# Gate weights turned by PE transposes beside the first attention units, and a drain of GpSimd in the half tile

## The chip, the cores and the metric

One core of one Trainium2 chip runs the whole kernel. A core has five engines with queues of their own: TensorE (PE, matmuls; PEld are its weight loads), VectorE (DVE), ScalarE (ACT), GpSimd (POOL) and SyncE (SP), which here only issues DMAs. POOL issues DMAs too, on a queue of its own. The metric is the device time of one execution in microseconds (us), smaller is better.

## What is computed

Three layers in a row, all in float32, for 4 x 448 = 1,792 tokens. Attention with a sigmoid in place of the softmax (12 heads of 64), then a layer with three weight matrices and an elementwise maximum, then a layer of 8 experts of which each token takes one:

```
attn = sigmoid(scale * q @ k.T - log(S));  x = attn @ v          # (1792, 768)
h = max(max(x @ w1, x @ w2), x @ w3);      x = h @ w_out         # 768 x 768 each
logits = x @ w_gate + modality_bias[modality_id]                 # w_gate: (768, 8)
e = argmax(logits);  gate = softmax(logits)[e]
out = gate * (relu(x @ ew1[e]) @ ew2[e])                         # 768 -> 1024 -> 768
```

## The kernel before

PE works through four stages in order: attention, the three projections (line 457), the output product (line 523), and the experts (lines 775 and 796, then the half tile, lines 928 and 938). Float32 products are made as three products of rounded parts: each operand is split into a rounded part and the rest, which is what the many pairs of a copy and a subtraction are for (`split_qk`, `split`, `evac_X`).

The attention has 24 units of two heads, and its loop runs over 12 pairs j of them, with units A = 2j and B = 2j + 1, and once more to finish. In an iteration PE makes the scores of A (`emit_qk`), the product with v of the unit before (`emit_av`, line 320, and `emit_av_last`, line 328, for the last 64 rows of a pair), the last scores of the pair (`emit_qk_last`, line 310), the scores of B and the product of A. In between stand, in this order, the loads of units A + 4 and B + 4 on SP's queue (`load_qk`, line 254, and `load_v`), the splits of units A + 2 and B + 2 on DVE (`split_qk`, lines 275 and 276, which write `kq`), and, from j = 2 on, 2.5 us of `background` work: the loads of the projection weights (`load_chunk`, line 216, tiles `stage`) and their conversion on DVE. PE, ACT, DVE and SP run in exactly the order written (`tc.manual_schedule`); POOL's order is the framework's, its waits too.

In iteration j = 4 SP issues four more transfers, of which the second is a transpose of the gate weights by a DMA of single elements, from `w_gate` (768 x 8) to `wgT` (8 x 768) in DRAM. `wgT` is read much later: `gate_load(e)`, in the projections, reads one row for all partitions, and DVE multiplies `w_out` with it, so that the logits can be had from `h` ahead of the output product. `mb` is the bias of the modalities, broadcast to 128 partitions, and `midi` is the modality of each token, 1,792 numbers of 8 bytes. The memory that the change uses is `K1`: before, it holds `v4`, the v of two units, and later `gk`, which is three times 768 columns.

At the end, the last tile of the experts has 128 rows (the half tile, i = NF). Its first products stand at line 928, its second products at line 938, and POOL scatters its rows to `out` (`scatter`, line 804), as it did those of the tile before. A loop over further tiles (line 949) isn't entered with these inputs. What the engines do at the program's end is shown under line 1000.

Of the kernel before, what the change touches and what calls it, by code (L numbers as in the profile page):

```python
# [28 lines left out]
def attn_moe_kernel(  # L29
# [15 lines left out]
    nc = tc.nc  # L45
    B, HP, D, _, _, S = qk.shape
    NT, DM = out.shape
    E, _, FF = ew1.shape
    KB = DM // 128
# [25 lines left out]
    def hold(tag, name, *shape):  # L75
        return pool.tile([128, *shape], F32, tag=tag, name=name)

    def r(ap):
        return ap.bitcast(F32R)

    def cut(a, off, *shape):

        n = 1
        for s in shape:
            n *= s
        a = a[:, off:off + n]
        if len(shape) == 2:
            a = a.rearrange("p (a b) -> p a b", a=shape[0])
        elif len(shape) == 3:
            a = a.rearrange("p (a b c) -> p a b c", a=shape[0], b=shape[1])  # L90
        return a
# [10 lines left out]
    NW = 2 * NJ  # L102
# [5 lines left out]
    kq = [cut(kq_, 4 * S * i, 2, 2, S) for i in range(2)]  # L108
    u1, u2, u3 = (hold(f"U{i}", f"u{i}", 2048) for i in range(3))
    qk_in = [cut(u, 2 * S * i, 2, S) for u in (u1, u2) for i in range(2)]  # L110
    v4 = hold("K1", "v4", 2, NW + 1, D)
    v_in = [cut(u3, (NW + 1) * D * i, NW + 1, D) for i in range(4)] + [v4[:, i] for i in range(2)]

    stage = [hold(f"S{i}", f"stage{i}", KB * 256).bitcast(I32) for i in range(2)]
# [7 lines left out]
    wgT = dram.tile([E, DM], F32, name="wgT")  # L122
# [3 lines left out]
    ident = cpool.tile([128, 128], F32, name="ident")  # L126
# [21 lines left out]
    def ps(tag, shape, name):  # L148
        return psum.tile(shape, F32, tag=tag, name=name)
# [3 lines left out]
    def ps_a(shape, name):  # L153
        a_n[0] ^= 1
        return psum.tile(shape, F32, tag=f"a{a_n[0]}", name=name)
# [54 lines left out]
    def load_chunk():  # L210
        i = loaded[0]
        if i < len(chunks):
            kind, a, b = chunks[i]
            loaded[0] += 1
            src, n = chunk_src(a, b) if kind == "w" else (woi[a * 128:(a + 1) * 128, :].rearrange("p (a c) -> p a c", a=1), 1)
            nc.sync.dma_start(out=stage[i % 2].rearrange("p (a c) -> p a c", a=n), in_=src)  # L216
# [34 lines left out]
    def load_qk(u):  # L251
        b, hp = divmod(u, HP)
        for h in range(2):
            nc.sync.dma_start(out=qk_in[u % 4][D * h:D * (h + 1)], in_=qk[b, hp, :, h])  # L254

    def load_v(u):
        b, hp = divmod(u, HP)
        vt = v_in[u % 6]
        if u % 2 == 0:
            nc.sync.dma_start(out=vt, in_=v[b, hp])  # L260
            return

        nc.sync.dma_start(out=vt[:, 0:NW], in_=v[b, hp, :, 0:NW])
        for h in range(2):
            nc.sync.dma_start(out=vt[SR * (1 - h):SR * (2 - h), NW], in_=v[b, hp, SR * h:SR * (h + 1), NW])

    def split_qk(u):
        src, kt = qk_in[u % 4], kq[u % 2]
        if u == 0:
            nc.vector.tensor_copy(out=r(kt[:, 0, 0]), in_=src[:, 0])  # L270
            nc.scalar.activation(out=r(kt[:, 0, 1]), in_=src[:, 1], func=ACTF.Copy)
            for i in range(2):
                nc.vector.tensor_tensor(out=r(kt[:, 1, i]), in0=src[:, i], in1=kt[:, 0, i], op=ALU.subtract)
        else:
            nc.vector.tensor_copy(out=r(kt[:, 0]), in_=src)  # L275
            nc.vector.tensor_tensor(out=r(kt[:, 1]), in0=src, in1=kt[:, 0], op=ALU.subtract)
# [3 lines left out]
    def scores():  # L280
        s_n[0] += 1
        return ps(("a0", "a1", "t")[s_n[0] % 3], [128, 2, 512], "s")

    def sigmoid(dst, s):
        nc.scalar.activation(out=dst, in_=s[:, :, 0:S], func=ACTF.Sigmoid, scale=qscale, bias=nlns)  # L285

    def emit_qk(u):

        kt = kq[u % 2]
        for g in range(NJ):  # L290
            s = scores()
            for n, (a, x) in enumerate(((0, 0), (0, 1), (1, 0))):
                for h in range(2):
                    p = slice(D * h, D * (h + 1))
                    nc.tensor.matmul(s[:, h, 0:S], r(kt[p, a, 0, 128 * g:128 * (g + 1)]), r(kt[p, x, 1]),  # L295
                                     start=(n == 0), stop=(n == 2))
            sigmoid(atb[u % 2][:, 2 * g:2 * g + 2], s)

    def quarter(i, h):

        return slice(SR * (h ^ i), SR * ((h ^ i) + 1))

    def emit_qk_last(j):

        s = scores()
        for i in range(2):
            src = qk_in[(2 * j + i) % 4]
            for h in range(2):
                p = slice(D * h, D * (h + 1))
                nc.tensor.matmul(s[quarter(i, h), i, 0:S], src[p, 0, 128 * NJ:], src[p, 1], start=True, stop=True)  # L310
        sigmoid(atl[j % 2], s)
# [3 lines left out]
    def emit_av(u):  # L315
        X_t[u] = ps(f"x{u % 2}", [128, 512], "X")
        vt, at = v_in[u % 6], atb[u % 2]
        for g in range(NJ):
            for h in range(2):
                nc.tensor.matmul(X_t[u][64 * h:64 * h + 64, 0:S], vt[:, 2 * g + h], at[:, 2 * g + h],  # L320
                                 start=(g == 0), stop=False)

    def emit_av_last(j):
        for i in range(2):
            u = 2 * j + i
            for h in range(2):
                p = quarter(i, h)
                nc.tensor.matmul(X_t[u][64 * h:64 * h + 64, 0:S], v_in[u % 6][p, NW], atl[j % 2][p, i],  # L328
                                 start=False, stop=True)

    def evac_X(u):
        b, hp = divmod(u, HP)
        src = X_t.pop(u)[:, 0:S]
        dR = xR[hp][:, b * S:(b + 1) * S]
        dL = xL[hp][:, b * S:(b + 1) * S]
        nc.vector.tensor_copy(out=r(dR), in_=src)
        nc.vector.tensor_tensor(out=r(dL), in0=src, in1=dR, op=ALU.subtract)

    with tc.manual_schedule(engines={mybir.EngineType.PE, mybir.EngineType.Activation, mybir.EngineType.DVE, SP}):
        load_qk(0)  # L340
        nc.vector.memset(gw, 0.0)
        nc.vector.memset(ones, 1.0)
        make_identity(nc, ident)
# [35 lines left out]
        for j in range(NU // 2 + 1):  # L379
            A, B, more = 2 * j, 2 * j + 1, j < NU // 2  # L380
            if more:
                emit_qk(A)
            if j:
                emit_av(B - 2)
                emit_av_last(j - 1)
                evac_X(A - 2)
                evac_X(B - 2)
            if not more:
                break
            emit_qk_last(j)  # L390
            for u in (A + 4, B + 4):
                if u < NU:
                    load_qk(u)
                    load_v(u)
            if A + 2 < NU:
                split_qk(A + 2)
            if j == 1:
                load_chunk()
            if j == 4:
                nc.sync.dma_start(out=slots.rearrange("(p c) o -> p (c o)", p=128), in_=idx)  # L400
                with nc.allow_non_contiguous_dma(reason="small"):
                    nc.sync.dma_start(out=wgT, in_=w_gate.rearrange("d e -> e d"))
                nc.sync.dma_start(out=mb, in_=m_bias.partition_broadcast(128))  # L403
                nc.sync.dma_start(out=midi, in_=mid.bitcast(I32).rearrange("(i p t) -> p i t", p=128, t=2))
            if j >= 2:
                background(2.5, stop=(1, 0))
            emit_qk(B)
            emit_av(A)
            if B + 2 < NU:
                split_qk(B + 2)  # L410
# [491 lines left out]
        for p, (i, n) in enumerate(todo[:NF * NCH]):  # L902
# [9 lines left out]
            else:  # L912
                f = n - 2 * KB
# [10 lines left out]
        for g in range(2):  # L924
            acc = ps_a([128, 4, 128], "hacc1")
            for f in range(4):
                for kk in range(KB):
                    nc.tensor.matmul(acc[:, f], raw[i % 2][0][kk // 2][:, kk % 2, 128 * (4 * g + f):128 * (4 * g + f + 1)],
                                     ht[:, kk], start=(kk == 0 and f == 0), stop=(kk == KB - 1 and f == 3))
            dR, dL = hv[0][:, 4 * g:4 * g + 4], hv[1][:, 4 * g:4 * g + 4]  # L930
            nc.scalar.activation(out=r(dR), in_=acc, func=ACTF.Relu)
            nc.vector.scalar_tensor_tensor(out=r(dL), in0=acc, scalar=0.0, in1=dR, op0=ALU.max, op1=ALU.subtract)
        o = [ps("t", [128, 512], "oh0"), ps("x0", [128, 512], "oh1")]
        for f in range(FB):
            w = bufs.pop((i, 2 * KB + f))
# [5 lines left out]
        d = xo[xo_n[0] % 3]  # L941
# [7 lines left out]
    with tc.For_i(NSTAT, nreg, 1) as iv:  # L949
        nc.sync.dma_start(out=idx2, in_=slots.rearrange("(p c) o -> p (c o)", p=128)[:, bass.ds(iv * 2, 2)])  # L950
        nc.sync.dma_start(out=e_dyn, in_=exd[0:1, bass.ds(iv, 1)])
        e = nc.values_load(e_dyn[0:1, 0:1], engines=(SP,), min_val=0, max_val=E - 1)
# [51 lines left out]
```

## Time and profile before

| | |
|---|---|
| median of 3 runs | 807.19 us (807.14 to 807.71) |
| the profiled execution | 807.75 us, its span 806.0 us |
| mean granted clock of TensorE | 0.974 |
| busy: PE, DVE, ACT, POOL | 760.3, 448.5, 258.6, 65.2 us |
| DMA | 88.04 MB, mean 109 GB/s |
| DMAs that POOL issues | 59: 14 to `slots`, 30 gathers to `xg`, 15 scatters to `out` |

The span is the time from the first to the last instruction that the profile shows. The 40 slices of the page are 20.15 us each; a digit is the busy share in tenths, and 9 is 90% or more. A matmul's end is modelled, so a busy PE is not a PE at its peak. In a timeline a row is: start us, duration us, engine, line, operation, tiles (out<-in), shapes, count, and in brackets the idle time before it and what ended it. An engine's name with a q (SPq, POOLq) is its sequencer: a long row there is an instruction that stood waiting.

### The profile page before, as it was taken

What the parts mean: (1) busy time and instruction counts of PE and PEld (TensorE: products, weight loads), DVE (VectorE), ACT (ScalarE), POOL (GpSimd) and SP (SyncE); (2) the same over time, 40 slices, a digit from 0 to 9 for tenths busy, and PEclk for the clock granted to TensorE, in tenths of its full rate; (3) what the DMA queues carried; (4) which work ended last, traced back from release to release, by engine and by line L of the source; (5) the groups of instructions that cost most, each with busy time, mean ns of one, the idle gap of its engine ahead of it and who ended that gap; (6) DMA issues with size and microseconds to landing.
All of it is one profiled execution on the core that took longest, in us unless ns stands there. A gap on an engine that the chain in (4) does not pass through costs nothing.

```text
span 806.0 us, 11821 instructions
## 1 busy us (share of the span) xinstructions
PE 760.3 (94%) x4698; PEld 642.0 (80%) x4698; DVE 448.5 (56%) x751; ACT 258.6 (32%) x362; POOL 65.2 (8%) x82
## 2 busy tenths in 40 slices
PE   9998059999999999999999999999999999999994
PEld 5454034479999999999997888998999999899993
DVE  3685047666696878784305822246665466555532
ACT  5665025520101010010003323245544445454522
POOL 0000000000000000000010060230220302021000
PEclk9999569999999999999999999999999999999998
DMA  8767596313242131220000196343657401064000
GB/s 206 206 148 2 3 225 164 109 40 118 77 153 83 59 117 59 79 79 1 0 1 1 54 368 243 102 144 133 249 171 263 157 22 59 14 246 148 20 25 18
DMA packets 50920, 88.04 MB, mean 109 GB/s; under 512 B 14219, under 2 KB 32908, under 8 KB 50862
## 3 DMA queue, kind: packets, MB, share of 16 engines
q1 hardware_dynamic: 47294, 75.71, 33.1%
q0 software_dynamic: 3568, 11.54, 4.3%
q8 instruction: 39, 0.64, 0.3%
q14 instruction: 19, 0.16, 0.1%
HBM read 94.95 MB, written 11.57 MB: 132 GB/s over the span
## 4 chain that ended last, share of the span: by engine, by line
PE 87%; SPq 6%; issue 2%; DMA 2%; DVE 1%; POOL 0%; ACT 0%; POOLq 0%; DVEq 0%
PE acc L457 33%; PE oacc L796 15%; PE hacc L775 14%; PE acc L523 7%; PE X L320 6%; PE s L295 5%; SPq L403 4%; PE acc2b L523 4%; DMA u<-in_qk_dram 2%; PE X L328 1%; PE xT L736 1%; PE s L310 1%; SPq L254 1%; PE lgp L483 1%; SPq L216 1%
## 5 line engine op out<-in xcount | busy, mean ns | idle before, releaser
L457 PE MATMUL acc<-xR,w_ring 128*128 128x448 f32 x864 | 210.5, 365 | 0.0
L457 PEld LDWEIGHTS acc<-xR,w_ring 128*128 128x128 f32 x864 | 162.2, 188 | 13.5 <-issue 0.7
L796 PE MATMUL oacc<-wo_ck,xh 128*128 128x512 f32 (+1 forms) x672 | 124.0, 340 | 0.0
L775 PE MATMUL hacc<-xh,wo_ck 128*128 128x256 f32 x1008 | 122.3, 283 | 0.0
L775 PEld LDWEIGHTS hacc<-xh,wo_ck 128*128 128x128 f32 x1008 | 121.9, 192 | 0.3
L796 PEld LDWEIGHTS oacc<-wo_ck,xh 128*128 128x128 f32 x672 | 102.8, 188 | 13.8
L285 ACT ACTIVATE at<-s,nlns 128x896 f32<-128x896 f32 x84 | 78.2, 1008 | 80.8 <-PE s L295 51.3
L457 PE MATMUL acc<-xLa,w_ring 128*128 128x448 f32 x360 | 102.2, 365 | 0.0
L295 PE MATMUL s<-kq 64*128 64x448 f32 x432 | 53.7, 388 | 31.8 <-DVE kq L275 31.2
L295 PEld LDWEIGHTS s<-kq 64*128 64x128 f32 x432 | 38.8, 190 | 54.2 <-issue 39.7
L182 DVE TENSOR_TENSOR wo_ck<-raw,wo_ck 128x512 fp32r<-128x512 f32 (+1 forms) x108 | 75.4, 743 | 6.0 <-ACT wo_ck L181 5.8
L523 PE MATMUL acc<-wo_ck,hs 128*128 128x512 f32 x252 | 77.4, 394 | 0.0
L457 PEld LDWEIGHTS acc<-xLa,w_ring 128*128 128x128 f32 x360 | 67.6, 188 | 5.3
L181 ACT ACTIVATE wo_ck<-raw 128x512 fp32r<-128x512 f32 (+1 forms) x108 | 67.0, 671 | 11.5 <-PE hacc L775 11.3
L523 PEld LDWEIGHTS acc<-wo_ck,hs 128*128 128x128 f32 x252 | 47.2, 188 | 11.4 <-ACT wo_ck L181 0.8
L523 PE MATMUL acc2b<-wo_ck,hs 128*128 128x256 f32 x252 | 56.2, 280 | 0.0
L439 DVE SCALAR_TENSOR_TENSOR gk<-wof,gk 128x768 f32<-128x768 f32 x48 | 45.9, 956 | 1.2
L461 ACT ACTIVATE hA<-acc 128x896 f32<-128x896 f32 x8 | 7.4, 920 | 115.1 <-PE acc L457 115.1
L782 DVE SCALAR_TENSOR_TENSOR xh<-hacc,xh 128x1024 fp32r<-128x1024 f32 x14 | 17.1, 1224 | 46.3 <-ACT xh L781 46.3
L727 POOL DMA_INDIRECT xg<-x2d,idx x30 | 30.0, 1000 | 148.2 <-PE xT L736 101.0
L523 PEld LDWEIGHTS acc2b<-wo_ck,hs 128*128 128x128 f32 x252 | 41.5, 189 | 0.1
L320 PE MATMUL X<-at,u 128*64 128x448 f32 x192 | 40.4, 557 | 0.0
(175 smaller groups left out, 666.5 us busy)
## 6 DMA issues: line engine op xcount, KB each, us to landing
raw<-in_moe_w_dram SPq DMA_DIRECT2D x24, 1024.0 KB
stage<-in_moe_w_dram SPq DMA_DIRECT2D x18, 768.0 KB
u<-in_qk_dram SPq DMA_DIRECT2D x48, 224.0 KB
raw<-in_moe_w_dram SPq DMA_DIRECT2D x12, 768.0 KB
raw_S<-in_moe_w_dram SPq DMA_DIRECT2D x12, 768.0 KB
stage<-in_moe_w_out_dram SPq DMA_DIRECT2D x6, 768.0 KB
x2d<-xo SPq DMA_DIRECT2D x14, 256.0 KB
gk<-wgT SPq DMA_DIRECT2D x8, 384.0 KB
```

What stands on the lines that cost most here:

```text
L181: nc.scalar.activation(out=r(dR), in_=src, func=ACTF.Copy)
L182: nc.vector.tensor_tensor(out=r(dL), in0=src, in1=dR, op=ALU.subtract)
L285: nc.scalar.activation(out=dst, in_=s[:, :, 0:S], func=ACTF.Sigmoid, scale=qscale, bias=nlns)
L295: nc.tensor.matmul(s[:, h, 0:S], r(kt[p, a, 0, 128 * g:128 * (g + 1)]), r(kt[p, x, 1]), start=(n == 0), stop=(n == 2))
L320: nc.tensor.matmul(X_t[u][64 * h:64 * h + 64, 0:S], vt[:, 2 * g + h], at[:, 2 * g + h], start=(g == 0), stop=False)
L403: nc.sync.dma_start(out=mb, in_=m_bias.partition_broadcast(128))
L439: nc.vector.scalar_tensor_tensor(out=junk, in0=wof[kb], scalar=1.0, in1=wgb[e % 2], op0=ALU.mult, op1=ALU.mult, accum_out=gw[:, kb, e:e + 1])
L457: nc.tensor.matmul(acc[:, c, 0:S], r(m[:, a, kk, :]), r(x[kk][:, c0 + S * c:c0 + S * (c + 1)]), start=(kk == 0 and n == 0), stop=(kk == KB ...
L523: nc.tensor.matmul(acc_t[t, c], r(hs[t][:, a, kk, :]), r(wo_rl[c][:, kk, b]), start=(kk == 0 and n == 0), stop=(kk == KB - 1 and n == 2))
L727: nc.gpsimd.indirect_dma_start(out=xg[i % 2][s][:, XC[c][0]:XC[c][1]], out_offset=None, in_=x2d[c], in_offset=bass.IndirectOffsetOnAxis(ap ...
L775: nc.tensor.matmul(acc[:, f], r(w[a][:, 128 * f:128 * (f + 1)]), r(x[:, kk]), start=(kk == 0 and m == 0 and f % 2 == 0), stop=(kk == KB - ...
L796: nc.tensor.matmul(dst, r(x[:, f, 128 * s:128 * (s + 1)]), r(w[a][:, c0:c1]), start=(f == 0 and m == 0 and not (shared and s == 1)), stop= ...
```

## The change

The transposing DMA on SP's queue goes. In its place POOL loads `w_gate` as it lies, in six blocks of 128 rows, at the start; after the last scores of the first pair PE transposes the six blocks into two PSUM tiles (`x0` and `x1`, which the products with v use next), DVE copies them to eight partitions of `K1`, and POOL stores them to `wgT`. `K1` becomes one tile with three parts. Apart from that, a drain of GpSimd is issued between the first and the second products of the half tile, at that place in POOL's order.

```
-    v4 = hold("K1", "v4", 2, NW + 1, D)
+    k1 = hold("K1", "k1", 3 * DM)
+    v4 = cut(k1, 0, 2, NW + 1, D)
+    wg_in = cut(k1, 2 * (NW + 1) * D, KB, E)
+    wg_t = k1[0:E, 2 * DM:3 * DM]
...
+    def turn_gate():
+
+        for x, k0, k1 in ((0, 0, 4), (1, 4, KB)):
+            T = ps(f"x{x}", [128, 512], "wgp")
+            for k in range(k0, k1):
+                nc.tensor.transpose(T[0:E, 128 * (k - k0):128 * (k - k0 + 1)], wg_in[:, k], ident)
+            nc.vector.tensor_copy(out=wg_t[:, 128 * k0:128 * k1], in_=T[0:E, 0:128 * (k1 - k0)])
+        nc.gpsimd.dma_start(out=wgT, in_=wg_t)
...
         load_qk(0)
+        nc.gpsimd.dma_start(out=wg_in, in_=w_gate.rearrange("(k p) e -> p k e", p=128))
         nc.vector.memset(gw, 0.0)
...
             emit_qk_last(j)
+            if not j:
+                turn_gate()
             for u in (A + 4, B + 4):
...
                 nc.sync.dma_start(out=slots.rearrange("(p c) o -> p (c o)", p=128), in_=idx)
-                with nc.allow_non_contiguous_dma(reason="small"):
-                    nc.sync.dma_start(out=wgT, in_=w_gate.rearrange("d e -> e d"))
                 nc.sync.dma_start(out=mb, in_=m_bias.partition_broadcast(128))
...
             nc.vector.scalar_tensor_tensor(out=r(dL), in0=acc, scalar=0.0, in1=dR, op0=ALU.max, op1=ALU.subtract)
+        tc.keep_in_program_order(nc.gpsimd.drain())
         o = [ps("t", [128, 512], "oh0"), ps("x0", [128, 512], "oh1")]
```

## Rows read from the trace of the kernel before

**Rows 1.** The page: PE's busy share in 40 slices.

```profile
PE   9998059999999999999999999999999999999994
```

**Rows 2.** The chain that ended last, whole span: start us, us, what.

```profile
44.00 2.41 PE X L320 x12
...
94.50 5.39 SPq L254
...
108.59 0.64 DVE kq L275
...
110.40 3.35 PE s L295 x16
...
120.74 2.40 PE X L320 x12
...
131.32 2.41 PE X L320 x12
...
168.63 262.86 PE acc L457 x1296
...
549.70 0.44 PE xT L736 x4
```

**Rows 3.** Waits, 78 to 112 us: who for whom, us, times, longest.

```profile
DVE kq L275 <- DMA u<-in_qk_dram: 33.2, 1, 33.2
```

**Rows 4.** Timeline, 50 to 120 us, around the hole.

```profile
58.09 0.81 SPq L402 DMA_DIRECT2D wgT<-in_moe_w_gate_dram  x1
...
58.95 30.48 SPq L403 DMA_DIRECT2D mb<-n_moe_modality_bias_dram  x1
...
75.67 2.48 PE L320 MATMUL X<-at,u 128*64 128x448 f32 x12
...
89.47 0.43 SPq L404 DMA_DIRECT2D midi<-in_moe_modality_id_dram  x1
```

**Rows 5.** DMA view, 60 to 90 us.

```profile
DMA packets 5982, 0.08 MB, mean 3 GB/s; under 512 B 5966, under 2 KB 5978, under 8 KB 5981
```

**Rows 6.** Line 1000: count, ns min/median/max, first to last start us.

```profile
L1000 POOLq DRAIN  x3: 103/179/4883, 799.9 to 805.6; - x3
...
L1000 PEldq DRAIN  x2: 8/8/8, 800.2 to 805.1; - x2
```

**Rows 7.** DMA view, 95 to 100 us: packets, MB, share of 16 engines.

```profile
q1 hardware_dynamic: 1862, 0.03, 38.5%
```

**Rows 8.** Timeline, 0 to 30 us: the first units.

```profile
0.83 2.50 SPq L254 DMA_DIRECT2D u<-in_qk_dram  x4
...
5.26 0.39 DVE L270 CAST kq<-u 128x448 fp32r<-128x448 f32 x1 [3.96 <-DMA u<-in_qk_dram]
...
7.86 1.09 DVE L276 TENSOR_TENSOR kq<-u,kq 128x896 fp32r<-128x896 f32 x1
...
9.63 0.50 PEld L295 LDWEIGHTS s<-kq 64*128 64x128 f32 x6 [0.70 <-ACT at L285]
9.63 2.63 PE L295 MATMUL s<-kq 64*128 64x448 f32 x18
...
10.64 0.63 DVE L275 CAST kq<-u 128x896 fp32r<-128x896 f32 x1 [1.68 <-PE s L295]
```

**Rows 9.** POOL's scatters to `slots`, line 689: issue ns, then us to landing.

```profile
L689 POOL DMA_INDIRECT slots<-tokid,spos x14: 954/958/1136, 464.2 to 481.0; - x14
...
DMA to landing us min/median/max: 5.0/6.0/6.7
```

**Rows 10.** Timeline, 775 to 810 us: POOL's last two scatters.

```profile
777.73 0.98 POOL L804 DMA_INDIRECT out_dram<-xo,idx  x1 [0.30 <-issue]
...
795.79 0.98 POOL L804 DMA_INDIRECT out_dram<-xo,idx  x1 [17.07 <-ACTq L949]
```

**Rows 11.** POOL's scatters to `out`, line 804: issue ns, then us to landing.

```profile
L804 POOL DMA_INDIRECT out_dram<-xo,idx x15: 982/1017/1552, 565.2 to 795.8; - x15
...
DMA to landing us min/median/max: 2.4/3.1/7.4
```

## The prediction

> **What bounds the kernel now.** I read the page first. TensorE (PE) is in the ninth tenth of nearly every slice; the exceptions are slices 5 and 6 (80 to 120 us), with 0 and 5, and the last with 4 [rows 1]. So only those two places can give much back: a hole in the attention stage, and the end.
>
> For the hole I read the chain of waits. The attention runs in periods: a block `X L320` stands at 120.74 and at 131.32, one period of 10.58 us later; before the hole it stands at 44.00 [rows 2]. Four periods after 44.00 is 86.32, and the block comes at 120.74: the hole costs 120.74 - 86.32 = 34.4 us, the cold clock behind it included. The list of waits says what was missing: VectorE waited 33.2 us for a load of `u`, the q and k of unit 14, before it could split them into `kq` [rows 3].
>
> The timeline of SyncE's queue (SP) says why the load was late. Behind the issue of `wgT` at 58.09 the next issue, that of `mb`, occupies the queue from 58.95 for 30.48 us; `midi` follows at 89.47 [rows 4]. The loads of unit 14, due in the next period near 63, are issued from 94.50 on [rows 2]. Which transfer blocked? From 60 to 90 us the DMA view counts 5,982 packets with 0.08 MB in all, nearly all under 512 B [rows 5]. `wgT` is 768 x 8 = 6,144 single elements of 4 B, `mb` 128 rows. So `wgT` is what drains there, and `mb` only stands behind it.
>
> **The end.** The last scatter is issued at 795.79 for 0.98 us, yet the span goes to 806.0. The rows of line 1000, the program's end, show why: PE, the last of the other engines, arrives at 800.2, and its drains last 8 ns; the longest of the three drains of GpSimd (Pool) starts at 799.9 and lasts 4,883 ns, to 804.8. Pool's other two last 103 and 179 ns [rows 6].
>
> **The change, part by part.**
>
> *Removed: the transposing `wgT` on SP.* Its drain of some 31 us goes, and at most the whole 34.4 us come back. The periods on both sides of the hole are PE's own, and from 168.63 PE runs line 457 for 262.86 us without a break [rows 2], so an earlier end of the attention carries through to the end of the kernel.
>
> *Left in the place: `mb` and `midi`.* `midi` has 1,792 runs of 8 B, and the loads of unit 14 are queued behind it. From its issue at 89.47 [rows 4] to the split that the load releases at 108.59 [rows 2] 19.1 us pass, with a stage load of 768 KB in them. Without `wgT`, `mb` takes its slot at 58.09 and `midi` goes out at about 58.7. The same 19.1 us later the load is there, at 77.8, and PE's long run on it starts 1.8 us after that (108.59 to 110.40 [rows 2]), at 79.6, with 2 of 18 matmuls done, worth 0.25. PE would want it at 75.67 + 2.48 = 78.15 [rows 4]. So 1.2 us of a hole stay. Bounds: 0, if the queue is faster with less behind it; 5.1, if the 1,792 runs cost 30.48/6,144 = 5.0 ns each like those of `wgT`, 8.9 us, against the 5 us in which they passed from 95 to 100 [rows 7]. I take 1.2, as the order of this queue is that of the trace.
>
> *Added: the gate load on Pool at the start.* 768 runs of 32 B compete with the loads of unit 0, on which everything waits (SP issues them from 0.83, VectorE gets them at 5.26 [rows 8]). Between 95 and 100 us 1,862 small packets took 38.5% of 16 engines, 1.9 us of them all [rows 7]; 768 are 0.8 us. Bounds 0 and 0.8; I take 0.4, since part of unit 0 is through before.
>
> Does it land in time? The transposes stand in PE's order behind `emit_qk_last(0)`, at 9.63 [rows 8]. Pool's 14 scatters of 128 four-byte rows ran beside a busy SP queue: 0.96 us each to issue, 5.0 to 6.7 us to landing [rows 9]. If Pool issues as early as SP, at about 0.85, this gives 6 to 7.6: no wait. If the issue grows with the rows, 6 x 0.96 = 5.7 us, it lands at 0.85 + 5.7 + (4.0 to 5.7) = 10.6 to 12.3: a wait of up to 2.7. I take 0.3, nearer to the rows as they stand.
>
> *Added: 6 transposes on PE, two copies on VectorE.* Four 128-column transposes take 0.44 us [rows 2], six 0.66. PE's weight loads wait 0.70 us for ScalarE's sigmoids at this place [rows 8], which may hide them: 0 to 0.7, I take 0.3. The copies, of 512 and 256 columns, are bounded by the 0.63 us that 896 columns take there, 1.3 for both. They stand ahead of `split_qk(2)`, which began at 10.64 and is wanted only at 14.7, after the 18 matmuls of 9.63 (to 12.26) and a block `X` of 2.48 [rows 4, 8]: hidden. If that cover is gone, 1.3.
>
> *Added: the store of `wgT` by Pool.* It goes out behind the copies, at 11 to 12 us; its readers belong to the projections, from 168.63 [rows 2], so over 150 us cover it. Of Pool's work behind it in its order the first that is wanted is `idx`, for the store of `slots` just ahead of 58.09 [rows 4]. On SP one issue less, 0.8 us in a place that then waits for nothing.
>
> *Added: the drain.* It stands in Pool's order between the scatters at 777.73 and 795.79 [rows 10]: 17 us without work on Pool, which would hide 4.9 us three times over. What it takes from the last drain this trace cannot show. Lower bound 0: the 4.88 us are a fixed price of the last drain. Upper bound: they are a working off of all the DMAs that Pool issued before, and with one left the drain costs what the two others cost, 0.1 to 0.2; then PE's arrival at 800.2 sets the end, and Pool goes on at about 800.25 instead of 804.8: 4.55 us. For the upper end: the two other drains, with no DMA since the one before, are some thirty times shorter. Against it: nothing in the trace shows what Pool does from 799.9 to 804.8. I take 4.55, as the short drains are the nearest rows. The Trainium skill speaks against it: "VectorE: DVE Perf Modes", "The DRAIN you can't avoid", has the drains at a program's ends constant, about 12 ns, on all five engines, so that an early one would change nothing, and the sum would stay at 32.2. PE's 8 ns agree with that, Pool's 4,883 ns do not [rows 6].
>
> **Sum**, against the profiled execution (807.75 us, 1.75 of it around the span): 34.4 - 1.2 - 0.4 - 0.3 - 0.3 = 32.2, and 4.55: 36.75 less, 771.0. That execution is 0.56 above the median of 807.19, so I forecast 770.4.
>
> **The rivals.**
> 1. *The drain gives nothing*: 807.19 - 32.2 = 775.0. For it: one long drain alone is seen, so a fixed price of the first drain at the end fits too. Against: the two short ones. Chance 0.20.
> 2. *`midi` holds unit 14 longer*: 3.9 us more at its bound, 774.3. For it: its runs are nearly as small as those of `wgT`, and behind it SP's issue at 94.50 stood for 5.39 us [rows 2]. Against: 5 us were enough for them [rows 7]. Chance 0.10.
> 3. *The gate weights come late, and PE stands in its order.* If Pool's issue reaches into VectorE's busy stretch (5.26 to 8.95 [rows 8]) and is held to its end, the load lands 2.4 to 3.1 us later [rows 11], at 11.4 to 12.1; PE waits 1.8 to 2.5, about 1.9 more than in the sum: 772.3. For it: 768 rows are six times what Pool issues elsewhere. Against: up to 5.26 VectorE has little to do. No row here shows such a collision. Chance 0.09. The Trainium skill, "SBUF — State Buffer", "SBUF: two separate sides", has this as a rule: GpSimd can't write its descriptors while VectorE runs an operation on both ports; no run here shows it so far.
> 4. *Slower*: the same place, at another size. Everything on PE stands behind the first transpose, so each us that the gate weights land after 9.6 costs one; past 46 us the change has lost all of its 36.7, and a landing at 50 gives 811. Against it: the slowest of Pool's 15 result scatters landed 7.4 us after its issue [rows 11]. Chance 0.02.
> 5. *SP stays blocked, as `mb` and not `wgT` was the cause*: 807.2 - 4.55 + 1.0 = 803.6. The count of packets speaks against it [rows 5]. Chance 0.02.
>
> The forecast has 0.57, and its own range is 768.2 (both parts whole, nothing paid) to 772.5. For 8 in 10 I reach up to 775.3, which takes in a drain without effect and most of 2 and 3. 0.2% is 1.6 us, about what a measurement of this kernel can tell from no change: faster 0.97 (all but rival 4 and oddities), same 0.01, slower 0.02.
>
> **What would show it.** In the changed profile SP's issue of `mb` should be short, PE's hole near 78 us under 2 us, line 457 should begin near 136 (168.6 - 32.2), the transposes should run by 10 us, and Pool's longest drain at line 1000 should be under 0.5 us, with one of some 5 us near 779 instead. I am wrong if a second hole follows `midi`, if PE waits for the gate weights, or if the last drain keeps its 4.9 us.

## The result and the profile after

| | before | after |
|---|---|---|
| median, 4 runs each | 807.16 us (806.36 to 807.71) | 769.75 us (769.36 to 769.87) |
| span of the profiled execution | 806.0 us | 767.6 us |
| projections begin (line 457, then 470) | 168.63 us | 134.72 us |
| from there to the end of the span | 637.4 us | 632.9 us |
| longest drain of GpSimd at the program's end | 4.88 us | 0.155 us |

The ratio is 0.9536 (95% interval 0.952 to 0.9553): faster by 37.4 us; 770.4 was forecast. The two lower parts of the table split the 38.4 us of the two spans: 33.9 lie before the projections begin, 4.5 behind.

The hole is gone from the page. Its row of PE's 40 slices, now of 19.19 us each, answers to [rows 1]; slices 5 and 6 have 9, and the last has 6 for 4:

```profile
PE   8999999999999999999999999999999999999996
```

In the chain of the changed kernel (start us, us, what) the same block stands 0.52 us later than the 44.00 of [rows 2], and the projections begin 33.9 us earlier:

```profile
44.52 2.41 PE X L323 x12
...
134.72 262.86 PE acc L470 x1296
```

PE's granted clock came back with it: before, it was 0.50 from 108 to 110 us and 0.61 from 110 to 117, behind 28 us without a matmul (80 to 108 us), that is at the lower of its two levels, 1.2 GHz, and then between the two; in the changed kernel it is 1.00, the upper level of 2.4 GHz, from 110 to 117.

The timeline around the place of the old hole, to be read beside [rows 4]. `mb` is issued in 0.65 us where it took 30.48, the loads of unit 14 are issued at 63.60 without standing (1.11 for two), their split at 75.84 waits for nothing, and PE's 18 matmuls on it at 78.58 follow the block of 76.17 at once:

```profile
58.60 0.65 SPq L416 DMA_DIRECT2D mb<-n_moe_modality_bias_dram  x1
...
59.29 0.43 SPq L417 DMA_DIRECT2D midi<-in_moe_modality_id_dram  x1
...
63.60 1.11 SPq L257 DMA_DIRECT2D u<-in_qk_dram  x2
...
75.84 0.62 DVE L278 CAST kq<-u 128x896 fp32r<-128x896 f32 x1
...
76.17 2.48 PE L323 MATMUL X<-at,u 128*64 128x448 f32 x12
...
78.58 2.09 PE L298 MATMUL s<-kq 64*128 64x448 f32 x18
```

The timeline of the start, beside [rows 8]. Unit 0 reaches VectorE at 5.54 (5.26 before). The six transposes run from 9.91, behind the scores of the last rows, and no wait stands in their row; the copies take 1.01 us on VectorE; the next scores begin at 10.66 instead of 9.63. Of this 1.03 us half is made good, since the waits for ScalarE there fall away: 2.12 us for 18 matmuls in place of 2.63.

```profile
5.54 0.39 DVE L273 CAST kq<-u 128x448 fp32r<-128x448 f32 x1 [4.25 <-DMA u<-in_qk_dram]
...
9.91 0.82 PE L339 MATMUL wgp<-ident,k 128*8 128x128 f32 x6
...
10.55 1.01 DVE L340 COPY k<-wgp 8x512 f32<-8x512 f32 x2 [1.15 <-PE wgp L339]
...
10.66 2.12 PE L298 MATMUL s<-kq 64*128 64x448 f32 x18
```

At the program's end (line 1014 now; count, ns min/median/max, first and last start), beside [rows 6]:

```profile
L1014 POOLq DRAIN  x3: 52/131/155, 766.0 to 767.4; - x3
...
L1014 PEldq DRAIN  x2: 8/8/8, 766.4 to 767.1; - x2
```

No drain there is long any more; PE's arrival at 766.4 sets the end. The early drain, in the view of its line, starts to wait at 743.5 and ends at 749.8, 5.0 us after the issue of the scatter ahead of it was done at 744.8, and 12 us before the last scatter:

```profile
L946 POOLq DRAIN  x1: 6338/6338/6338, 743.5 to 743.5; - x1
```

### The profile page after: what moved, and what is told of

It is laid out like the page before. It is cut to its first block, busy times and chain, and to the rows that moved or that the text cites. A ratio compares the mean times of both kernels' runs of the same rounds, so it can differ in the third digit from the quotient of the medians.

```text
span 767.6 us, 11841 instructions
## 1 busy us (share of the span) xinstructions
PE 757.6 (99%) x4704; PEld 641.1 (84%) x4704; DVE 449.2 (59%) x753; ACT 258.4 (34%) x362; POOL 67.6 (9%) x84
## 4 chain that ended last, share of the span: by engine, by line
PE 97%; DMA 1%; DVE 0%; issue 0%; POOL 0%; POOLq 0%; ACT 0%; SPq 0%; DVEq 0%
PE acc L470 34%; PE oacc L809 15%; PE hacc L788 15%; PE acc L536 8%; PE X L323 8%; PE s L298 6%; PE acc2b L536 4%; PE X L331 1%; PE hacc L941 1%; PE s L313 1%; PE xT L749 1%; PE oh L952 1%; PE lgp L496 1%; DMA u<-in_qk_dram 1%; DMA x2d<-xo 0%; DMA xg<-x2d,idx 0%
## 5 line engine op out<-in xcount | busy, mean ns | idle before, releaser
L184 ACT ACTIVATE wo_ck<-raw 128x512 fp32r<-128x512 f32 (+1 forms) x108 | 67.0, 671 | 11.6 <-PE hacc L788 11.4
L298 PE MATMUL s<-kq 64*128 64x448 f32 x432 | 51.2, 377 | 0.7 <-DVE kq L276 0.5
```

The lines of the kernel that those rows point to most:

```text
L184: nc.scalar.activation(out=r(dR), in_=src, func=ACTF.Copy)
```

## The experiments

The three batches ran on chips of their own, on which the kernel before took 816.9, 817.0 and 809.8 us; so ratios are compared across batches, and of the profiles the times of single steps. From the start of the projections to the end of the span the changed kernel takes 637.2 us on the second of these chips, and the kernel before with the drain alone 637.6 on the first, against 632.9 above: these 4 us more come with the chip and not with the change. The theory after the result: the single elements cost the wait of what stands behind them, and a drain of GpSimd works off the DMAs issued before it. The rivals: the elements hold the DMA engines whoever issues them; the last drain has a fixed price.

**gate_only: the changed kernel without the drain.**

```
-        tc.keep_in_program_order(nc.gpsimd.drain())
```

> The changed kernel without the early drain of GpSimd: the gate weights alone. If the two parts are independent, the attention keeps all it won (the projections begin near 134.7 us as in the changed kernel, 33.9 earlier than before) and the last drain of GpSimd is long again, 4.9 us for some 61 DMAs: 769.75 + 4.5 = 774.3 us. If the early drain was no part of the gain (the last drain short anyway, because no transfer of single elements has gone before), the time stays at 769.8.

779.02 us against 816.94: ratio 0.9532 (0.95 to 0.9564). The last drain is long again:

```profile
L1013 POOLq DRAIN  x3: 46/237/5050, 772.9 to 779.0; - x3
```

The profiled execution took 781.02 us, the other three 778.64 to 779.36; in it the projections begin at 136.91 us, 2.2 later than in the changed kernel. Unit 0 came at 6.24 here, 0.7 later; PE had stood for 1.43 us before the first scores, and its granted clock from 7 to 12 us was 0.66, between its two levels of 1.2 and 2.4 GHz, where the changed kernel had 1.00. In the chain the first scores take 3.35 us for 16 matmuls, in the changed kernel 1.89:

```profile
7.89 3.35 PE s L298 x16
```

**drain_only: the kernel before with the drain alone.**

```
+        tc.keep_in_program_order(nc.gpsimd.drain())
         o = [ps("t", [128, 512], "oh0"), ps("x0", [128, 512], "oh1")]
```

> The kernel before with nothing but the early drain. Theory of a backlog: the early drain takes about 5 us in GpSimd's idle stretch, the last one falls from 4.88 to under 0.2 us, and the time to 807.16 - 4.5 = 802.6 us. Rival, a fixed price of the last drain: 807.2 us and a last drain of 4.9 us.

812.35 us: ratio 0.9939 (0.9919 to 0.996), 4.6 us less. The drains at the end, then the early one:

```profile
L1001 POOLq DRAIN  x3: 51/103/136, 811.5 to 812.7; - x3
```

```profile
L933 POOLq DRAIN  x1: 6160/6160/6160, 789.1 to 789.1; - x1
```

A fixed price of the last drain is refuted. The hole is untouched here, and on this chip it is longer (projections from 175.41 us, 38.5 behind those of gate_only), which is why the gate part alone brings as much in this batch as both parts did in the first measurement.

**after_again: the changed kernel on the second chip.**

> The changed kernel again, on the chip of this batch, so that the batch has its own yardstick. If the two parts add up, its ratio is 0.9532 less the 0.0056 to 0.0061 that the drain alone brought, about 0.947 on a chip with a hole as long as in the first batch, and 0.9536 on one like that of the first measurement. The last drain under 0.2 us.

773.32 us against 817.0: ratio 0.9471 (0.9431 to 0.9512). The product of the two parts alone is 0.9532 x 0.9939 = 0.9474: they add up. The projections begin at 134.80 us, as in the first measurement.

**elem_pool: who issues the elements.**

```
-                    nc.sync.dma_start(out=wgT, in_=w_gate.rearrange("d e -> e d"))
+                    nc.gpsimd.dma_start(out=wgT, in_=w_gate.rearrange("d e -> e d"))
```

> The kernel before, with its transfer of 6,144 single elements issued by GpSimd instead of SP and nothing else changed; GpSimd issues it at about 2.6 us. Theory: the hole came from SP's order alone, in which the loads stood behind the elements; then no load stands behind them here, PE has no hole of more than 2 us, the projections begin near 135 us, and the time is about 773 us. Rival: the 4-byte packets hold the 16 DMA engines themselves, whoever issued them; then the first loads are held for up to some 30 us and the time is about 800 us.

One run: 820.42 us, and the projections begin at 180.15. The hole is not gone, it has moved to where GpSimd now issues the elements, the start, where PE waits for the loads of the first units; so the run changes the place along with the queue. The page's row of PE:

```profile
PE   6437999999999999999999998999999999999995
```

and the DMA view from 8 to 50 us (packets, MB, share of 16 engines):

```profile
q1 hardware_dynamic: 590, 1.17, 66.6%
q0 software_dynamic: 201, 0.05, 14.6%
```

GpSimd's queue is q0 here. SP's queue q1 moves 1.17 MB in 42 us (8.28 MB in the same stretch of the kernel before), beside 0.05 MB of elements, though nothing of it stands behind them in SP's order. My theory fell: it is not the order of one queue alone. The rival, that the elements hold the engines, forecast this hole, if a shorter one. A packet of q1 took 42 x 16 x 0.666/590 = 0.76 us on average in this stretch, so q1's own packets were slow too; what they share with the elements beyond the engines, the trace doesn't say.

**elem_sbuf: where the elements go.** They stay on SP in their place, but go to SBUF, and GpSimd stores the rows.

```
-                    nc.sync.dma_start(out=wgT, in_=w_gate.rearrange("d e -> e d"))
+                    nc.sync.dma_start(out=wg_t, in_=w_gate.rearrange("d e -> e d"))
+                nc.gpsimd.dma_start(out=wgT, in_=wg_t)
```

> The kernel before, with the transfer of single elements still in its place on SP but written to eight partitions of SBUF instead of DRAM, and from there stored to DRAM by GpSimd as in the changed kernel; no transposes on PE, no copies, no drain. Theory: what was slow is the writing of 4-byte pieces to DRAM (5.3 ns each), since the 1,792 runs of 8 bytes of midi went to SBUF in about 1.2 us in the changed kernel; then the 6,144 elements take some 5 to 10 us and the hole is 0 to 8 us: 774 to 782 us. Rival: each element has its price wherever it is written, the hole stays near 34 us and the time at 807 us.

785.94 us: ratio 0.9609 (0.9573 to 0.9645). The timeline:

```profile
59.92 11.88 SPq L406 DMA_DIRECT2D mb<-n_moe_modality_bias_dram  x1
...
71.84 0.43 SPq L407 DMA_DIRECT2D midi<-in_moe_modality_id_dram  x1
...
83.48 0.63 DVE L277 CAST kq<-u 128x896 fp32r<-128x896 f32 x1 [7.99 <-DMA u<-in_qk_dram]
...
84.25 0.74 PE L297 MATMUL s<-kq 64*128 64x448 f32 x2 [6.03 <-DVE kq L277]
```

The issue behind the elements stands 11.88 us, not 30.48 or the 32.54 of drain_only on the same chip. So with SBUF as the destination the next issue stands some 60% less; the rest remains and leaves PE a hole of 6.0 us. The time falls by 31.0 of the 37.9 us that gate_only wins on this chip. Between 61 and 72 us 5,828 packets pass, 1.9 ns each:

```profile
DMA packets 5828, 0.04 MB, mean 4 GB/s; under 512 B 5827, under 2 KB 5827, under 8 KB 5827
```

**elem_late: what stands behind the elements.** The same transfer on SP to DRAM, after the last attention loads:

```
-                    nc.sync.dma_start(out=wgT, in_=w_gate.rearrange("d e -> e d"))
...
+        with nc.allow_non_contiguous_dma(reason="small"):
+            nc.sync.dma_start(out=wgT, in_=w_gate.rearrange("d e -> e d"))
         background(99, stop=(1, 0))
```

> The kernel before, with its transfer of 6,144 single elements still on SP and to DRAM, but issued after the last attention loads. What stands behind it then are the loads of projection weights. Theory that its price is the wait of what stands behind: no hole in the attention (the projections begin near 134.2 us, 0.5 earlier than in the changed kernel, which pays for the transposes), but VectorE, in order, waits for weights behind some 31 us of elements, and PE for VectorE: 10 to 30 us come back as a hole in the projections. Rival: the weights are loaded far enough ahead; then no hole anywhere, and the span is about 0.5 us below that of the gate part alone.

One run: 775.5 us against 809.84. The timeline, the waits from 130 to 400 us, and the chain's last stretch of line 457:

```profile
110.28 1.05 SPq L410 DMA_DIRECT2D wgT<-in_moe_w_gate_dram  x1
111.44 28.29 SPq L216 DMA_DIRECT2D stage<-in_moe_w_out_dram  x1
```

```profile
DVE cv L165 <- DMA stage<-in_moe_w_out_dram: 11.6, 1, 11.6
...
PEld acc L457 <- DVE hA L463: 2.2, 1, 2.2
```

```profile
158.25 241.03 PE acc L457 x1188
```

The elements hold a load of weights for 28 us, VectorE waits 11.6 us for it, and PE some 2 us at 158. The forecast hole of 10 to 30 us was too large: PE had matmuls until 156.4, and VectorE, late by its wait, freed PE's next accumulator at 158.2 (`hA`, line 463). The projections began at 134.25 us, as forecast. So nearly all of the 34.4 us is a matter of what waits for the transfers that the elements slow down; placed among loads with time to spare they cost 2 us.

**turn_early: the transposes ahead of the first scores.**

```
         split_qk(1)
+        turn_gate()
         for j in range(NU // 2 + 1):
...
-            if not j:
-                turn_gate()
```

> The changed kernel with the transposes ahead of the first scores instead of behind them. In the changed kernel the gate weights had landed at 5.9 us, and PE waits at 6.6 to 7.2 us for the split of unit 0 in any case. Theory: 0.25 of the 0.5 us that the start costs are the transposes, the other part is the later landing of unit 0; then the projections begin at about 134.45 instead of 134.7 us. Rival: PE stands in its order for the gate weights, and they begin later than 134.7.

One run: 770.15 us. The timeline has the wait that the rival named, and the projections begin at 135.24 (chain), 0.5 later than in the changed kernel:

```profile
6.11 0.81 PE L339 MATMUL wgp<-ident,k 128*8 128x128 f32 x6 [0.50 <-DMA k<-in_moe_w_gate_dram]
...
6.30 0.39 DVE L273 CAST kq<-u 128x448 fp32r<-128x448 f32 x1 [5.01 <-DMA u<-in_qk_dram]
...
6.92 0.19 PEld L298 LDWEIGHTS s<-kq 64*128 64x128 f32 x2 [0.29 <-ACT kq L274]
```

But that wait is not what made it late. Unit 0 itself reached VectorE at 6.30 in this execution, 0.76 later than in the changed kernel, and the first scores, at 6.92, waited for its split and not for the transposes. Counted from that split the projections begin 128.94 us later here, and 129.16 to 129.20 in the seven other profiles with the gate load (gate_only, with its low clock, left out). So the 0.24 us of the transposes is saved, as the theory had it, and the half microsecond lost is unit 0's landing. That landing varies: 5.45 to 6.30 us in the nine profiles with the gate load, 5.26 to 5.38 in the five without. One run doesn't show whether the new place has a part in the 6.30.

**drain_mid: the early drain three tiles forward.**

```
                 finish(i, ixs[i])
+                if i == 3:
+                    tc.keep_in_program_order(nc.gpsimd.drain())
...
-        tc.keep_in_program_order(nc.gpsimd.drain())
```

> The changed kernel with the early drain moved three tiles forward, to the end of tile 3, so that about 12 DMAs of GpSimd follow it instead of 1. Backlog of DMAs at 83 ns each: the moved drain takes about 4.1 us (49 of 61) and the last one about 1.0 us. Fixed price of whichever drain comes last but one: the last drain stays at 0.13 us. Fixed price of the last drain: 4.9 us.

One run: 774.65 us. At the end, with 12 DMAs behind the early drain:

```profile
L1015 POOLq DRAIN  x3: 52/155/1029, 770.6 to 772.6; - x3
```

1.03 us, as the backlog of 83 ns each has it. The moved drain, behind 49 DMAs, ends at 649.6, 4.1 us after the issue ahead of it was done (645.4), as forecast too. Both fixed prices are refuted.

**extra_rows1, extra_rows128, and the same with 60: more DMAs, small or larger, on top of gate_only.** `xtra` are DRAM tiles that nobody reads.

```
+    xtra = [dram.tile([128, E], F32, name=f"more{i}") for i in range(30)]
...
+        for m in xtra:
+            nc.gpsimd.dma_start(out=m[0:1, :], in_=bias_t[0:1, 0])
```

> The gate part alone (no early drain), and 30 more DMAs of GpSimd between attention and projections, each a store of one row of 32 B to DRAM that nobody reads. Backlog by count of DMAs: 91 of them, the last drain 5.05 + 30 x 0.083 = 7.5 us, the time 2.5 us above that of the gate part alone. Backlog by rows or bytes: the drain stays at about 5.1 us.

```profile
L1017 POOLq DRAIN  x3: 46/103/7500, 770.8 to 778.9; - x3
```

> The same 30 more DMAs with 128 rows of 32 B each. By count of DMAs: 7.5 us again. By rows (some 7,550 rows in 59 DMAs before, 0.65 ns each): 5.05 + 3,840 x 0.65 ns = 7.5 us too, while one row each gave 5.1. If old DMAs are also worked off when room for new ones is needed, as the 3.17 us after the transfer of 6,144 elements by GpSimd suggest, less than with one row each, possibly below 5 us.

 (There `m[0:128, :]` and `bias_t[:, 0]`.)

```profile
L1017 POOLq DRAIN  x3: 46/103/7500, 770.8 to 778.8; - x3
```

7.500 us both times, in 780.98 and 780.89 us: the count of DMAs sets the drain here, not rows or bytes. With 60 for 30:

> The gate part alone and 60 more stores of one row by GpSimd. By count of DMAs: 121 of them, the last drain 10.0 us.

```profile
L1017 POOLq DRAIN  x3: 46/103/9950, 766.9 to 777.4; - x3
```

> The same 60 with 128 rows each. By count alone 10.0 us as well. If GpSimd also works old DMAs off when it needs room for rows (3.17 us instead of 4.97 after the transfer of 6,144 elements), the drain is shorter than with one row each, perhaps 3 to 8 us.

```profile
L1017 POOLq DRAIN  x3: 46/103/1538, 766.6 to 768.7; - x3
```

9.95 us for 121 DMAs of which the extra ones are small, 1.54 us where they have 128 rows. So past some amount of rows the old DMAs are worked off without a drain, at a time that costs PE nothing here (770.73 us against 779.43 in the same batch). elem_pool points the same way, 3.17 us with 60 DMAs, one of 6,144 elements. That they go when room is needed fits these runs; where the limit lies, and what is done there, the runs don't show.

## Why the prediction was right

**The hole.** 34.4 us was read off the chain as the most that could come back. The attention now runs without a hole, and the whole came back less the 0.52 us of the start: 33.9. The reading that `wgT` drains and `mb` only stands behind it holds. That SP's order alone was the reason, as the prediction's wording implies, does not: elem_pool has the elements on another queue and still a hole. What the elements and the other queue's packets share stays open.

**What `midi` leaves.** 1.2 us was forecast, 0 came; this step failed. "The same 19.1 us later the load is there" carried over a time from a queue in trouble: before, 202 packets in all passed from 90 to 96 us, behind the issue of `midi`; in the changed kernel 1,523 passed from 61 to 62. That the empty stretch is the tail of the elements is inferred from this, not shown. In the changed kernel the load behind `midi` is issued at once, and the split at 75.84, 16.6 us after the issue of `midi`, had no wait. In elem_sbuf, where the elements ahead go to SBUF, 11.6 us pass from `midi` (71.84) to the split (83.48), and that one did wait. Rival 2 is out with it.

**The start.** Forecast 0.4 + 0.3 + 0.3 = 1.0 us, measured 0.52. Unit 0 comes 0.28 us later (0.4 forecast), but not by the working of 768 small packets: GpSimd's queue shows 32 packets up to 9 us, 0.2 us of the 16 engines, and in the other runs with the gate load unit 0 comes 0.2 to 1.0 us later than the 5.26 of the kernel before. That 0.28 came near 0.4 is in part luck. So 0.52 belongs to this execution; with the gate load the projections begin between 134.62 and 135.24 us, and at 136.91 where the clock fell (gate_only). Nobody waits for the gate weights in the changed kernel (0.3 forecast); Pool's issue took 1.02 us for 768 runs, within the 0.95 to 1.14 for 128 rows [rows 9], and was over long before VectorE's work on unit 0 began, so rivals 3 and 4 had no ground. The transposes took 0.82 us where 0.66 was worked out, of which 0.24 stayed (0.3 forecast; turn_early saves just that), the rest hidden by ScalarE's lag as argued.

**The drain.** 4.55 us forecast; 4.5 between the start of the projections and the end of the spans, 4.6 for the drain alone. PE's arrival sets the end, as worked out. The upper end rested on the two short drains, and the count of DMAs behind it is now shown: 4.88 us for 59 DMAs, 4.97 for 60 (elem_sbuf), 5.05 for 61, 7.50 for 91, 9.95 for 121, and 1.03 for 12: 82 to 86 ns each. The Trainium skill's sentence on drains at a program's ends, "VectorE: DVE Perf Modes", "The DRAIN you can't avoid", some 12 ns and constant on all five engines, holds in these runs for the four others (7 to 17 ns), not for GpSimd.

**The sum.** 32.2 + 4.55 = 36.75 forecast; the medians moved by 37.4 us. The two terms that were too dear, `midi` by 1.2 and the start by 0.5, account for the 38.4 of the spans with the drain's 4.5; the profiled executions are the upper of before and the lowest of after.

## What to carry to other kernels

Before moving a transfer of single elements to another queue, ask what has to move while it drains: here another queue, which also moved them to the start, brought nothing, a destination in SBUF some four fifths, a place with slack nearly all, and whole rows turned on PE all but half a microsecond in the measured run. A load added at the start is paid in the landing of the first unit, and that price differs from run to run. Look at the last drain of each engine at a program's end; if GpSimd's grows with the DMAs that it has issued, drain it once where it is idle, as late as its work allows, since what it issues afterwards is paid at the end. A time taken from a queue in trouble carries the trouble with it: price what remains behind a removed transfer by a stretch without it.

## What the runs showed of the hardware

- GpSimd's drain takes 82 to 86 ns for each DMA that it issued since the last one, the same with 30 extra DMAs of one row or of 128. With 60 extra of 128 rows it took 1.54 us after 121 DMAs, which fits earlier ones being settled without it.
- With 768 runs of 32 B loaded by GpSimd beside them, the first unit's loads reached VectorE at 5.45 to 6.30 us in nine profiles, at 5.26 to 5.38 in five without.
- 6,144 elements of 4 B from DRAM to DRAM held the next issue for 28.3 to 32.5 us, to eight partitions of SBUF for 11.9 us.
- Beside those elements on another queue SP's stream of loads fell to 1.17 MB in 42 us, from 8.28 MB without them.
